# Values of an attention kernel cast to bf16 by their DMA instead of by an engine, in a kernel that interleaves attention with an MLP

## The chip, the cores and the metric

One core of a Trainium2 chip runs the whole program. The metric is the device time of one execution in microseconds (us), the median of several runs. Engines: PE is TensorE, DVE is VectorE, ACT is ScalarE, POOL is GpSimd, SP is SyncE; "PEld" is PE's weight load, and "SPq" or "POOLq" is an engine's queue of DMA issues.

## The reference, cut to what matters

Attention over 8 batches with 8 heads of 576 positions and 64 features, then an MLP with a gate over all 4608 tokens:

```python
scores = (1/8) * q @ k.T
mask_plain = (rel >= 0) & (rel < 32)                          # heads 0 to 3
mask_dil   = (rel >= 0) & (rel < 128) & (rel % 4 == 0)        # heads 4 to 7
attn = softmax(where(mask, scores, -1e9));   y = attn @ v      # per batch and head
x = y.transpose(0, 2, 1, 3).reshape(4608, 512)
h = x @ w_in                                                  # 512 -> 2048
out = (h * sigmoid(beta * h)) @ w_out                          # 2048 -> 512
```

## The kernel before

Matmuls are in bf16. The MLP works on nine tiles of 512 tokens; while tile t is at the MLP, attention of batch t+1 is done in the same instruction streams. What the two share out is fixed when the program is built: each attention step has a **weight**, and a step is put behind the next MLP slot (four matmuls) as soon as the share of weights done falls behind the share of slots done. Batches 0, 1 and 2 have step lists of their own; batches 3 to 7 share one.

```python
THIRD = ("d0 d1 v0 S20 S21 S22 k0 S23 v1 V20 S30 k1 V21 S31 q0 V22 ... V33 v2 S10 V00 ...").split()  # batch 2
WORK = {"S": 3, "V": 3, "X": 2, "d": 3, "K": 3, "Q": 3, "k": 0, "q": 0, "v": 1}
...
while work and done * total < whole * seen:       # seen: MLP slots passed; tile 0 (batch 1) goes by a count of steps
    m, name = work.pop(0)
    done += WORK[name[0]]
    ...                                           # extras tied to this step (loads, spreads)
    attention_step(b, name)
```

S is scores and exp, V is the product with the values, X is the transposition into `xT`, the input of the MLP. The values go through f32 staging tiles and a cast:

```python
vp_st = [const([P, 4, NI, D], FP32) ...]          # plain heads, staged
vd_st = const([P, 2, 4, C, D], FP32)              # dilated heads, staged
vp[i], vd[i]                                      # bf16, rows of 66: 64 values, a column of ones, padding

def cast_v(b, n, eng):                            # after load_vp / load_vd into the staging tiles
    if n == 2 or n > 3:
        copy_on(eng)(out=vp[b % 2][:, h, :, 0:D], in_=vp_st[b % 2][:, h])
    else:
        copy_on(eng)(out=vd[b % 2][0:K, f]...[:, :, 0:D], in_=vd_st[0:K, f]...)
```

In batches 3 to 7 POOL casts; in batch 2 ACT does all of it (the steps v0, v1, v2); in batches 0 and 1 DVE, POOL and ACT share it. From the MLP the argument needs only that the product of `w_in` and `xT` follows the X steps of the batch on PE, in order, and that one DVE instruction per 128 features makes the gate product `g`:

```python
def slot_h(t, fb):
    for kt in (2, 3, 0, 1):                       # dilated columns of xT first, then the plain ones
        nc.tensor.matmul(hps, lhsT=w_in_bf[:, kt, ...], rhs=xT[:, kt, t*512:(t+1)*512], ...)
    nc.scalar.activation(out=tnh, in_=hps, func=ACT.Tanh, scale=beta_half)
    nc.vector.scalar_tensor_tensor(out=g, in0=tnh, scalar=1.0, in1=hps, op0=add, op1=mult)
```

The softmax here doesn't subtract the row's maximum and nothing guards it: scores larger than these inputs give would overflow.

Of the kernel before, what the change touches and what calls it, by code (L numbers as in the profile page):

```python
# [8 lines left out]
FP32 = mybir.dt.float32  # L9
BF16 = mybir.dt.bfloat16  # L10
# [10 lines left out]
).split()  # L21

FIRST = (
    "W10 K2 W2 Q2 W2 K3 S20 S21 Q3 W1 S22 S23 z0 S30 S31 S32 S33 v0 W2 V20 V21 K0 W1 v1 V22 K1 V23 W1 Q0 "
    "V30 W1 V31 W1 X20 S00 V32 S01 V33 X21 S02 v4 S10 X30 S11 V00 S12 X31 V01 H0 v5 X00 V10 H1 X01 V11 X10 X11 "
    "z1 z2"
).split()
SECOND = (
    "K2 Q2 K3 Q3 v0 S20 v1 S21 S22 S23 K0 K1 S30 V20 S31 Q0 V21 S32 V22 S33 V23 V30 S00 "
    "V31 X20 v2 S01 V32 S02 V33 S10 X21 S11 V00 X30 S12 V01 X31 V10 X00 V11 X01 X10 X11"  # L30
).split()
THIRD = (
    "d0 d1 v0 S20 S21 S22 k0 S23 v1 V20 S30 k1 V21 S31 q0 V22 S32 q1 V23 S33 q2 q3 V30 X20 S00 V31 "
    "S01 X21 V32 S02 V33 v2 S10 V00 X30 S11 V01 S12 X31 V10 X00 V11 X01 X10 X11"
).split()


# [1 line left out]
def kernel(  # L39
# [10 lines left out]
    nc = tc.nc  # L50
    P = 128
    B, H, S, D = q.shape
# [4 lines left out]
    WIN = 32  # L57
    C = 4
    CT = S // C
    DQ = (96, 48)  # L60
    DK = (96, 80)
    DO = (0, 64)
    QT = 96
    NI = S // QT
# [35 lines left out]
    const = lambda shape, dt, name: const_pool.tile(shape, dt, name=name)  # L100
    w_in_bf = const([P, NKT, DFF], BF16, "w_in_bf")
    w_out_bf = const([P, NFB, HD], BF16, "w_out_bf")
    ident_f = const([NFB, NFB], FP32, "ident_f")
# [16 lines left out]
    pt = [const([P, pt_w[x] + 80], BF16, f"pt{x}") for x in range(4)]  # L120
    vp = [const([P, 4, NI, DV], BF16, f"vp{i}") for i in range(2)]
    vd = [const([P, 2, 4, C, DV], BF16, f"vd{i}") for i in range(2)]
    vp_st = [const([P, 4, NI, D], FP32, f"vp_st{i}") for i in range(2)]
    vd_st = const([P, 2, 4, C, D], FP32, "vd_st")


    k1 = [xT[:, 2 * i:2 * i + 2, 2 * S:2 * S + WIN + S] for i in range(2)]
# [21 lines left out]
    def zeros():  # L149
        nc.vector.memset(warm_w[:], 0.0)  # L150
        nc.vector.memset(warm[:], 0.0)
        for hf in range(2):
            nc.vector.memset(neg_d[hf][:], 0.0)
        nc.vector.memset(neg_p[:], 0.0)
        nc.vector.memset(qzd[0][64:128, 0], 0.0)
        nc.vector.memset(qzd[0][0:64, 1], 0.0)
        nc.vector.memset(vp_st[0][0:WIN, 0, 0], 0.0)
        for x in range(4):
            nc.vector.memset(pt[x][:, pt_w[x]:], 0.0)
        for x in range(2, 4):  # L160
            nc.vector.memset(pt[x][64:96, 8 * DQ[0]:8 * DQ[0] + 32], 0.0)
        for i in range(2):
            nc.vector.memset(vd[i][:, :, :, :, D:D + 1], 1.0)
            nc.vector.memset(k1[i][:, :, 0:WIN], 0.0)
            nc.vector.memset(vp[i][:, :, :, D:D + 1], 1.0)
        nc.vector.memset(plain_T["k"][:, 0:WIN // 2], 0.0)
# [28 lines left out]
    def build_neg_p():  # L195
        band(neg_p[:], QT, -WIN, -1, 0.0, -NEG)
        nc.gpsimd.memset(neg_p[0:WIN, 0], -NEG)
# [31 lines left out]
    def load_w_in(c0, c1):  # L229
        nc.gpsimd.dma_start(  # L230
            out=w_in_bf[:, :, c0:c1], in_=moe_w_in[:, c0:c1].rearrange("(c p) d -> p c d", p=P))

    def load_w_out(g):
        nc.gpsimd.dma_start(
            out=w_out_bf[:, g * 4:(g + 1) * 4, :],
            in_=moe_w_out[g * 4 * P:(g + 1) * 4 * P, :].rearrange("(c p) d -> p c d", p=P))
# [32 lines left out]
    def load_plain(b, kind):  # L269
        r0 = H * S if kind == "q" else 0  # L270
        dst = raw[b, kind] = plain_T[kind]
        c0 = WIN // 2 if kind == "k" else 0
        nc.sync.dma_start_transpose(
            out=dst[:, c0:c0 + 2 * S],
            in_=scratch[b][r0:r0 + 4 * S].rearrange("(a r) d -> a (r d)", r=2))

    def copy_on(eng):
        return eng.copy if eng is nc.scalar else eng.tensor_copy
# [20 lines left out]

    def load_vp_1(b, eng, n=0, m=4 * NI, p=0):  # L300
        eng.dma_start(
            out=vp_st[b % 2][:].rearrange("p h i d -> p (h i) d")[p:P, n:n + m],
            in_=bass.AP(tensor=v.tensor, offset=v[b, 0].offset + (QT * n - WIN + p) * D,
                        ap=[[D, P - p], [QT * D, m], [1, D]]))


    def load_vp(b, eng, n=0, m=4 * NI, p=0):
        st = vp_st[b % 2][:].rearrange("p h i d -> p (h i) d")
        for e in range(2):
            eng.dma_start(  # L310
                out=st[64 * e + p:64 * e + 64, n:n + m],
                in_=bass.AP(tensor=v.tensor,
                            offset=v[b, 0].offset + (QT * n - WIN + e + 2 * p) * D,
                            ap=[[2 * D, 64 - p], [QT * D, m], [1, D]]))

    def load_vd(b, eng):
        rows = v[b, 4:8].rearrange("h (t T) d -> t h (T d)", T=C)
        st = vd_st[:].rearrange("p f h T d -> p f h (T d)")
        for hf in range(2):
            eng.dma_start(out=st[0:DK[hf], hf], in_=rows[DO[hf]:DO[hf] + DK[hf]])  # L320


    def cast_v(b, n, eng):
        if n == 2 or n > 3:
            h = slice(0, 4) if n == 2 else slice(2 * n - 8, 2 * n - 6)
            copy_on(eng)(out=vp[b % 2][:, h, :, 0:D], in_=vp_st[b % 2][:, h])
        else:
            f, K = (slice(n, n + 1), DK[n]) if n < 2 else (slice(0, 2), 96)
            copy_on(eng)(  # L329
                out=vd[b % 2][0:K, f].rearrange("p f h T e -> p (f h T) e")[:, :, 0:D],  # L330
                in_=vd_st[0:K, f].rearrange("p f h T d -> p (f h T) d"))


    for b in range(2):
# [139 lines left out]
            nc.scalar.copy(out=o, in_=xp[:, 0:m * n].rearrange("p (T t) -> p T t", T=C))  # L474

    STEP = {"K": step_k, "Q": step_q, "S": step_s, "V": step_v, "X": step_x}
    BRING = {"d": spread_dil, "k": spread_k, "q": spread_q, "v": cast_v, "z": zeros_q}

    def attention_step(b, name):
        if name[0] == "W":  # L480
            for n in range(int(name[1:])):
                nc.tensor.matmul(warm_ps[:], lhsT=warm_w[:, 0:P], rhs=warm_w[:], start=True, stop=True)
        elif name[0] == "H":
            early[0] = -1
            slot_h(0, int(name[1:]), (2, 3))
        elif name[0] in STEP:
            STEP[name[0]](b, *[int(c) for c in name[1:]])
        else:
            eng = (nc.scalar if name[0] == "v" and (b, name) in ((1, "v2"), (2, "v0"), (2, "v1"), (2, "v2")) else
                   nc.gpsimd if b == 0 and name in ("v1", "v4", "v5") else nc.vector)  # L490
            BRING[name[0]](b, int(name[1:]), eng)


    g_t, o_t = {}, {}
# [89 lines left out]
    def extras(b):  # L584
        e = {}
        at = lambda name, fn, *a: e.setdefault(steps(b).index(name), []).append(lambda: fn(*a))
        V, A, G = nc.vector, nc.scalar, nc.gpsimd
        SQ = nc.sync
        if b + 1 < B:
            if b > 1:  # L590
                if b == 2:
                    at("S20", gate, raw[2, "q"][0:1, 0:1])
                for kind in "kq":
                    at("S20", cast_qk, b + 1, kind)
                at("X20", load_vd, b + 1, SQ)
                at("X20", load_vp, b + 1, SQ)
            if b == 1:
                at("X20", load_vd, b + 1, SQ)
                at("X20", load_vp, b + 1, SQ)
            if b > 1:  # L600
                for kind in "kq":
                    at("V21", load_dil, b + 1, kind)
                for kind in "kq":
                    at("V30", load_plain, b + 1, kind)
            if b > 1:
                at("S11", spread_dil, b + 1, 0, V)
                at("V01", spread_dil, b + 1, 1, V)
                at("X00", cast_v, b + 1, 3, G)
                at("X01", cast_v, b + 1, 2, G)
        return e  # L610


# [17 lines left out]
    load_tok(0, "q", 0)  # L630
    load_vp_1(0, G, 0, 1, WIN)
    load_vp_1(0, G, 1, 2 * NI - 1)
    load_vp_1(0, G, 2 * NI, 2 * NI)
    for name in FIRST:
        if name == "v1":
            attention_step(0, "v1")
            build_neg_p()
            for c0, c1 in ((0, 256), (256, 512), (512, 1024)):
                load_w_in(c0, c1)
            continue  # L640
        if name == "v5":
            load_w_in(1024, 2048)
            make_identity(nc, ident_f[:])
        if name == "X10":
            build_beta()
        attention_step(0, name)
    for x, g in ((1, 0), (0, 1)):
        for n in "kq":
            load_tok(1, n, x)
        load_w_out(g)  # L650
    G.memset(vd_st[64:96, 1], 0.0)
    load_vd(1, G)
    load_w_out(2)
    load_vp_1(1, G)
# [3 lines left out]
        load_dil(2, kind)  # L658
    for kind in "kq":
        load_plain(2, kind)  # L660
    load_w_out(3)
    zeros_kz()
    build_masks_d()
# [1 line left out]


    at_once = [3, 2] + [1] * (NTT - 3) + [4]
    WORK = {"S": 3, "V": 3, "X": 2, "d": 3, "K": 3, "Q": 3, "k": 0, "q": 0, "v": 1}
    left = []
    first = lambda n: max(0, n - 9) if n < 14 else 3 * n - 37  # L670
    for t in range(NTT):
        slots = []
        n = len(left)
# [59 lines left out]
```

## Time and profile before

| before | |
|---|---|
| median of the first 3 runs | 334.56 us (333.59 to 335.07) |
| span of the profiled run | 332.6 us |
| busy over the span: PE, ACT, DVE, POOL | 314.1, 199.3, 193.9, 131.4 us |
| V casts on POOL, from batch 3 on | 3.35 us a batch |

PE bounds the kernel; the stages, the waits of PE and the casts are shown line by line in the prediction. The profile's list of DMA queues shows one thing more (packets, MB, share of 16 engines' span): the uncast values of batches 2 to 7 went through q1 (those of batches 0 and 1 were issued from POOL and went through q0).

```profile
q1 hardware_dynamic: 57264, 25.58, 39.7%
q0 software_dynamic: 7632, 16.64, 27.5%
```

### The profile page before, as it was taken

The page shows a single profiled execution, that of the slowest core. Times are in us where ns is not written, and L with a number is a line of the kernel's source. Part 1 is how long each engine was busy: PE and PEld are TensorE (multiplying, and loading weights), DVE is VectorE, ACT ScalarE, POOL GpSimd, SP SyncE. Part 2 cuts the span into 40 slices and gives each one's busy share as a digit, 9 for nine tenths or more (in the row PEclk, how much of TensorE's full clock was granted, in tenths as well). Part 3 has the DMA queues.
Part 4 walks back from the last instruction along what each step waited for, and adds up shares of the span by engine and source line. Part 5 has one row for each costly group of instructions (what it writes and reads, how often), then busy time and mean ns, then how long its engine had stood idle before and what let it go on. Part 6 is the DMA issues. An engine that isn't in the chain of part 4 may idle for free.

```text
span 332.6 us, 6335 instructions
## 1 busy us (share of the span) xinstructions
PE 314.1 (94%) x2382; PEld 168.8 (51%) x2426; DVE 193.9 (58%) x432; ACT 199.3 (60%) x382; POOL 131.4 (39%) x172
## 2 busy tenths in 40 slices
PE   7798999987899899999999999999999999999995
PEld 3564466544455455555555555555555544444444
DVE  4558775479657775777376737673766344344400
ACT  3576756685757666666666666666666545355511
POOL 8792693133385346533653365335533000000000
PEclk9879999999999999999999999999999999999999
DMA  6999999998799795889597959792011210011131
GB/s 112 205 184 196 223 249 184 206 211 204 145 157 178 124 188 113 156 200 149 102 176 170 148 102 175 178 139 64 3 34 32 63 34 33 32 34 32 32 95 65
DMA packets 64927, 42.63 MB, mean 128 GB/s; under 512 B 48896, under 2 KB 58784, under 8 KB 64512
## 3 DMA queue, kind: packets, MB, share of 16 engines
q1 hardware_dynamic: 57264, 25.58, 39.7%
q0 software_dynamic: 7632, 16.64, 27.5%
q8 instruction: 19, 0.31, 0.4%
q14 instruction: 12, 0.10, 0.1%
HBM read 39.32 MB, written 16.52 MB: 168 GB/s over the span
## 4 chain that ended last, share of the span: by engine, by line
PE 84%; DVE 5%; ACT 3%; DMA 2%; POOL 2%; issue 2%; POOLq 0%; ACTq 0%; DVEq 0%
PE h_ps L505 31%; PE o_ps L543 27%; PE at L543 5%; PE at L443 4%; PE at L460 3%; PE at L505 3%; DVE g L515 2%; DMA xT<-in_k_dram 2%; PE h_ps L543 2%; PE at L410 2%; PE at L417 2%; ACT tnh L512 1%; PE at L358 1%; DVE qq L294 1%; PE at L559 1%
## 5 line engine op out<-in xcount | busy, mean ns | idle before, releaser
L515 DVE SCALAR_TENSOR_TENSOR g<-tnh,h_ps 128x512 bf16<-128x512 bf16 x130 | 88.7, 684 | 89.4 <-ACT tnh L512 88.8
L505 PE MATMUL h_ps<-xT,w_in_bf 128*128 128x512 bf16 x504 | 129.5, 379 | 3.2 <-DVE g L515 2.1
L512 ACT ACTIVATE tnh<-h_ps,beta_half 128x512 bf16<-128x512 f32 x130 | 89.4, 687 | 55.8 <-PE h_ps L505 51.6
L543 PE MATMUL o_ps<-w_out_bf,g 128*128 128x512 bf16 x429 | 109.3, 379 | 1.0
L505 PEld LDWEIGHTS <-w_in_bf 128*128 128x128 bf16 x576 | 51.8, 98 | 52.2 <-issue 4.1
L543 PEld LDWEIGHTS <-g 128*128 128x128 bf16 x560 | 50.2, 98 | 47.5
L425 POOL TENSOR_TENSOR pt<-pt,mask_d 96x384 bf16<-96x384 bf16 (+1 forms) x48 | 36.7, 775 | 49.9 <-ACT pt L423 49.3
L423 ACT ACTIVATE pt<-at 128x384 bf16<-128x384 f32 (+2 forms) x107 | 46.0, 439 | 17.0 <-PE at L410 8.6
L450 DVE TENSOR_TENSOR xs<-at,rcp 48x256 bf16<-48x256 f32 (+2 forms) x91 | 42.2, 463 | 8.8 <-PE at L460 4.7
L425 POOL TENSOR_TENSOR pt<-pt,mask_PP 128x384 bf16<-128x384 bf16 x24 | 22.8, 951 | 37.5 <-ACT pt L423 37.4
L443 PEld LDWEIGHTS <-pt 128*128 128x128 bf16 (+2 forms) x448 | 24.8, 99 | 15.3 <-DVE vd L329 1.2
L548 ACT ACTIVATE osb<-o_ps 128x512 f32<-128x512 f32 x28 | 16.7, 597 | 19.0 <-PE o_ps L543 18.7
L446 DVE RECIPROCAL rcp<-at 48x4 f32<-48x4 f32 (+2 forms) x91 | 16.0, 176 | 7.8 <-PE at L443 7.1
L417 PEld LDWEIGHTS <-kdT 128*96 128x96 bf16 (+1 forms) x128 | 14.3, 120 | 10.8 <-issue 1.4
L460 PE MATMUL at<-ident_b,xs 96*128 96x96 bf16 (+1 forms) x224 | 18.1, 200 | 1.6 <-DVE xs L450 1.0
L543 PE MATMUL at<-w_out_bf,g 128*128 128x512 bf16 x79 | 19.3, 379 | 0.1
L460 PEld LDWEIGHTS <-xs 96*128 96x128 bf16 (+1 forms) x224 | 13.4, 97 | 11.3 <-issue 2.1
L443 PE MATMUL at<-vd,pt 96*128 96x65 bf16 (+1 forms) x244 | 17.7, 196 | 0.7 <-DVE vd L329 0.7
L417 PE MATMUL at<-qzd,kdT 128*80 128x96 bf16 (+1 forms) x122 | 17.1, 226 | 1.0 <-DVE qzd L282 1.0
L425 POOL TENSOR_TENSOR pt<-pt,mask_FP 128x384 bf16<-128x384 bf16 x12 | 10.9, 912 | 16.1 <-ACT pt L423 16.1
L505 PE MATMUL at<-xT,w_in_bf 128*128 128x512 bf16 x54 | 13.5, 379 | 0.8 <-DVE kdT L371 0.4
L474 ACT COPY xT<-at 128x384 bf16<-128x384 bf16 (+1 forms) x32 | 12.7, 396 | 2.6 <-PE at L460 2.6
(115 smaller groups left out, 259.1 us busy)
## 6 DMA issues: line engine op xcount, KB each, us to landing
vp_st<-in_v_dram SPq DMA_DIRECT2D x12, 384.0 KB, 9.2
qk<-in_k_dram POOLq DMA_DIRECT2D x6, 576.0 KB, 6.1
qk<-in_q_dram POOLq DMA_DIRECT2D x6, 576.0 KB, 9.3
vd_st<-in_v_dram SPq DMA_DIRECT2D x6, 384.0 KB, 5.7
w_out_bf<-in_moe_w_out_dram POOLq DMA_DIRECT2D x4, 512.0 KB, 16.2
vd_st<-in_v_dram SPq DMA_DIRECT2D x6, 320.0 KB, 6.7
out_dram<-osb SPq DMA_DIRECT2D x7, 256.0 KB, 2.9
out_dram<-osb SPq DMA_DIRECT2D x8, 224.0 KB, 2.4
```

The costliest lines, as they stand in the source:

```text
L417: nc.tensor.matmul(sc[0:K, a, 0:2 * n], lhsT=kd[b][:, rp, h4, DO[hf]:DO[hf] + K], rhs=qzd[b % 2][:, :, rp, h4, hf * DQ[0]:hf * DQ[0] + n], ...
L423: nc.scalar.activation(out=w, in_=sc[0:K, :, 0:2 * n], func=ACT.Exp, scale=SCALE)
L425: nc.gpsimd.tensor_tensor(out=w, in0=w, in1=mask[0:K], op=ALU.mult)
L443: nc.tensor.matmul(pv[:, a, h2, :], lhsT=pt[x][0:K, c:c + P], rhs=rhs, start=True, stop=True)
L446: nc.vector.reciprocal(out=rcp[0:n, 0:m], in_=pv[0:n, :, :, D])
L450: nc.vector.tensor_tensor(out=xs_t[b, x, jx][:, a0:a0 + m], in0=pv[0:n, :, :, 0:D], in1=rcp[0:n, 0:m].unsqueeze(3).to_broadcast([n, m, 2, ...
L460: nc.tensor.transpose(xp[:, a * n:(a + 1) * n], xs[:, a].rearrange("p h d -> p (h d)"), ident_b[0:n, 0:n])
L505: nc.tensor.matmul(hps, lhsT=w_in_bf[:, kt, fb * P:(fb + 1) * P], rhs=xT[:, kt, t * NTOK:(t + 1) * NTOK], start=(kt == 2), stop=(kt == 1))
L512: nc.scalar.activation(out=tnh[:], in_=hps, func=ACT.Tanh, scale=beta_half[:, fb:fb + 1])
L515: nc.vector.scalar_tensor_tensor(out=g[:], in0=tnh[:], scalar=1.0, in1=hps, op0=ALU.add, op1=ALU.mult)
L543: nc.tensor.matmul(ops[:], lhsT=g_t[t, fb][:, tb * P:(tb + 1) * P], rhs=w_out_bf[:, fb, :], start=(fb == 0), stop=(fb == NFB - 1))
L548: nc.scalar.mul(out=osb[:], in_=ops[:], mul=0.5)
```

## The change

The intent is to rid the engines of the casts: a DMA can turn f32 into bf16 on its way. Plain heads go straight into the padded tile, whose row of 64 values is 128 B at a stride of 132 B, so a load becomes 3072 pieces (24 per partition, 128 partitions) of 256 B read and 128 B written. Dilated heads go as rows of 1 KB into a bf16 staging tile, and a copy ("spread") puts them into the padded tile. All these loads are now issued from POOL. The core of the diff:

```diff
-    vp_st = [const([P, 4, NI, D], FP32, f"vp_st{i}") for i in range(2)]
-    vd_st = const([P, 2, 4, C, D], FP32, "vd_st")
+    vd_st = [const([P, 2, 4, C * D], BF16, f"vd_st{i}") for i in range(2)]
 # load_vp, load_vp_1: out=vp[...][p:P, n:n + m, 0:D] instead of vp_st
-    def cast_v(b, n, eng): ...
+    def spread_v(b, hf, eng):
+        copy_on(eng)(out=vd[b % 2][0:K, hf]...[:, :, 0:D], in_=vd_st[b % 2][0:K, hf]...)
 # THIRD: the steps v0, v1, v2 are gone (SECOND loses v2, FIRST loses v4 and v5)
-    WORK = {..., "v": 1}
+    WORK = {..., "v": 0}
 # extras of batch b, for batch b + 1:
-                at("X20", load_vd, b + 1, SQ); at("X20", load_vp, b + 1, SQ)
-                at("X00", cast_v, b + 1, 3, G); at("X01", cast_v, b + 1, 2, G)
+            if b == 1:
+                at("X20", load_vp, b + 1, G)
+                at("X10", spread_v, b + 1, 0, A); at("X11", spread_v, b + 1, 1, A)
+            if b > 1:
+                at("X20", load_vd, b + 1, G); at("X20", load_vp, b + 1, G)
+                at("X00", spread_v, b + 1, 0, G); at("X01", spread_v, b + 1, 1, G)
 # start-up: w_in is issued without waiting for a cast of vd; vd of batch 2 goes ahead of w_out's last quarter
+    load_vd(2, G)
     load_w_out(3)
```

More of the change, by code (lines that the diff above doesn't have):

```diff
@@ L23 @@
 FIRST = (
-    "W10 K2 W2 Q2 W2 K3 S20 S21 Q3 W1 S22 S23 z0 S30 S31 S32 S33 v0 W2 V20 V21 K0 W1 v1 V22 K1 V23 W1 Q0 "
-    "V30 W1 V31 W1 X20 S00 V32 S01 V33 X21 S02 v4 S10 X30 S11 V00 S12 X31 V01 H0 v5 X00 V10 H1 X01 V11 X10 X11 "
+    "W10 K2 W2 Q2 W2 K3 S20 S21 Q3 W1 S22 S23 z0 S30 S31 S32 S33 v0 W2 V20 V21 K0 v1 W1 V22 K1 V23 W1 Q0 "
+    "V30 W1 V31 W1 X20 S00 V32 S01 V33 X21 S02 S10 X30 S11 V00 S12 X31 V01 H0 X00 V10 H1 X01 V11 X10 X11 "
     "z1 z2"
@@ L28 @@
 SECOND = (
-    "K2 Q2 K3 Q3 v0 S20 v1 S21 S22 S23 K0 K1 S30 V20 S31 Q0 V21 S32 V22 S33 V23 V30 S00 "
-    "V31 X20 v2 S01 V32 S02 V33 S10 X21 S11 V00 X30 S12 V01 X31 V10 X00 V11 X01 X10 X11"
+    "K2 Q2 K3 Q3 v0 S20 S21 v1 S22 S23 K0 K1 S30 V20 S31 Q0 V21 S32 V22 S33 V23 V30 S00 "
+    "V31 X20 S01 V32 S02 V33 S10 X21 S11 V00 X30 S12 V01 X31 V10 X00 V11 X01 X10 X11"
 ).split()
 THIRD = (
-    "d0 d1 v0 S20 S21 S22 k0 S23 v1 V20 S30 k1 V21 S31 q0 V22 S32 q1 V23 S33 q2 q3 V30 X20 S00 V31 "
-    "S01 X21 V32 S02 V33 v2 S10 V00 X30 S11 V01 S12 X31 V10 X00 V11 X01 X10 X11"
+    "d0 d1 S20 S21 S22 k0 S23 V20 S30 k1 V21 S31 q0 V22 S32 q1 V23 S33 q2 q3 V30 X20 S00 V31 "
+    "S01 X21 V32 S02 V33 S10 V00 X30 S11 V01 S12 X31 V10 X00 V11 X01 X10 X11"
 ).split()
@@ L156, in zeros @@
         nc.vector.memset(qzd[0][0:64, 1], 0.0)
-        nc.vector.memset(vp_st[0][0:WIN, 0, 0], 0.0)
+        nc.vector.memset(vp[0][0:WIN, 0, 0, 0:D], 0.0)
         for x in range(4):
@@ L301, in load_vp_1 @@
         eng.dma_start(
-            out=vp_st[b % 2][:].rearrange("p h i d -> p (h i) d")[p:P, n:n + m],
+            out=vp[b % 2][:].rearrange("p h i d -> p (h i) d")[p:P, n:n + m, 0:D],
             in_=bass.AP(tensor=v.tensor, offset=v[b, 0].offset + (QT * n - WIN + p) * D,
@@ L307, in load_vp @@
     def load_vp(b, eng, n=0, m=4 * NI, p=0):
-        st = vp_st[b % 2][:].rearrange("p h i d -> p (h i) d")
+        st = vp[b % 2][:].rearrange("p h i d -> p (h i) d")
         for e in range(2):
             eng.dma_start(
-                out=st[64 * e + p:64 * e + 64, n:n + m],
+                out=st[64 * e + p:64 * e + 64, n:n + m, 0:D],
                 in_=bass.AP(tensor=v.tensor,
@@ L317, in load_vd @@
         rows = v[b, 4:8].rearrange("h (t T) d -> t h (T d)", T=C)
-        st = vd_st[:].rearrange("p f h T d -> p f h (T d)")
         for hf in range(2):
-            eng.dma_start(out=st[0:DK[hf], hf], in_=rows[DO[hf]:DO[hf] + DK[hf]])
-    def cast_v(b, n, eng):
-        if n == 2 or n > 3:
-            h = slice(0, 4) if n == 2 else slice(2 * n - 8, 2 * n - 6)
-            copy_on(eng)(out=vp[b % 2][:, h, :, 0:D], in_=vp_st[b % 2][:, h])
-        else:
-            f, K = (slice(n, n + 1), DK[n]) if n < 2 else (slice(0, 2), 96)
-            copy_on(eng)(
-                out=vd[b % 2][0:K, f].rearrange("p f h T e -> p (f h T) e")[:, :, 0:D],
-                in_=vd_st[0:K, f].rearrange("p f h T d -> p (f h T) d"))
+            eng.dma_start(out=vd_st[b % 2][0:DK[hf], hf], in_=rows[DO[hf]:DO[hf] + DK[hf]])
+    def spread_v(b, hf, eng):
+        K = DK[hf]
+        copy_on(eng)(
+            out=vd[b % 2][0:K, hf].rearrange("p h T e -> p (h T) e")[:, :, 0:D],
+            in_=vd_st[b % 2][0:K, hf].rearrange("p h (T d) -> p (h T) d", T=C))
     for b in range(2):
@@ L476 @@
     STEP = {"K": step_k, "Q": step_q, "S": step_s, "V": step_v, "X": step_x}
-    BRING = {"d": spread_dil, "k": spread_k, "q": spread_q, "v": cast_v, "z": zeros_q}
+    BRING = {"d": spread_dil, "k": spread_k, "q": spread_q, "v": spread_v, "z": zeros_q}
     def attention_step(b, name):
@@ L488, in attention_step @@
         else:
-            eng = (nc.scalar if name[0] == "v" and (b, name) in ((1, "v2"), (2, "v0"), (2, "v1"), (2, "v2")) else
-                   nc.gpsimd if b == 0 and name in ("v1", "v4", "v5") else nc.vector)
-            BRING[name[0]](b, int(name[1:]), eng)
+            BRING[name[0]](b, int(name[1:]), nc.vector)
     g_t, o_t = {}, {}
@@ L589, in extras @@
         if b + 1 < B:
+            if b == 1:
+                at("X20", gate, raw[2, "q"][0:1, 0:1])
+                at("X20", load_vp, b + 1, G)
+                at("X10", spread_v, b + 1, 0, A)
+                at("X11", spread_v, b + 1, 1, A)
             if b > 1:
-                if b == 2:
-                    at("S20", gate, raw[2, "q"][0:1, 0:1])
                 for kind in "kq":
                     at("S20", cast_qk, b + 1, kind)
-                at("X20", load_vd, b + 1, SQ)
-                at("X20", load_vp, b + 1, SQ)
-            if b == 1:
-                at("X20", load_vd, b + 1, SQ)
-                at("X20", load_vp, b + 1, SQ)
+                at("X20", load_vd, b + 1, G)
+                at("X20", load_vp, b + 1, G)
             if b > 1:
@@ L607, in extras @@
                 at("V01", spread_dil, b + 1, 1, V)
-                at("X00", cast_v, b + 1, 3, G)
-                at("X01", cast_v, b + 1, 2, G)
+                at("X00", spread_v, b + 1, 0, G)
+                at("X01", spread_v, b + 1, 1, G)
         return e
@@ L632 @@
     load_vp_1(0, G, 1, 2 * NI - 1)
+    build_neg_p()
     load_vp_1(0, G, 2 * NI, 2 * NI)
+    for c0, c1 in ((0, 256), (256, 512), (512, 1024), (1024, 2048)):
+        load_w_in(c0, c1)
+    make_identity(nc, ident_f[:])
     for name in FIRST:
-        if name == "v1":
-            attention_step(0, "v1")
-            build_neg_p()
-            for c0, c1 in ((0, 256), (256, 512), (512, 1024)):
-                load_w_in(c0, c1)
-            continue
-        if name == "v5":
-            load_w_in(1024, 2048)
-            make_identity(nc, ident_f[:])
         if name == "X10":
@@ L650 @@
         load_w_out(g)
-    G.memset(vd_st[64:96, 1], 0.0)
     load_vd(1, G)
@@ L667 @@
     at_once = [3, 2] + [1] * (NTT - 3) + [4]
-    WORK = {"S": 3, "V": 3, "X": 2, "d": 3, "K": 3, "Q": 3, "k": 0, "q": 0, "v": 1}
+    WORK = {"S": 3, "V": 3, "X": 2, "d": 3, "K": 3, "Q": 3, "k": 0, "q": 0, "v": 0}
     left = []
```

## The prediction

> **What bounds the kernel now.** I read the summary first, then its 40 slices, then a table of busy time by stage, and only then the waits inside each stage. TensorE (PE) is busy 94% of the span, and the chain of work that ended last is 84% PE. So the question is not how much other work the change removes but where PE stands still. These are the stages (columns: stretch, its length, busy us with instruction counts of PE, PEld, DVE, ACT, POOL, then granted clock, DMA share, GB/s):
>
> ```profile
> 0.00:30.00 30.00, 24.41 (x279) 15.53 (x283) 17.04 (x61) 16.28 (x38) 21.57 (x41) 0.89 1.02 174
> 30.00:60.00 30.00, 28.90 (x292) 16.79 (x296) 20.85 (x44) 20.25 (x39) 17.91 (x26) 1.00 1.17 213
> 60.00:100.00 40.00, 34.99 (x282) 18.80 (x287) 26.34 (x58) 27.68 (x55) 17.08 (x21) 1.00 0.98 184
> 100.00:130.00 30.00, 28.47 (x229) 15.46 (x231) 22.12 (x48) 20.19 (x41) 15.17 (x17) 1.00 0.83 149
> 130.00:310.00 180.00, 178.58 (x1205) 92.33 (x1229) 104.39 (x218) 109.55 (x204) 59.63 (x68) 1.00 0.51 99
> 310.00:332.60 22.60, 18.74 (x102) 9.89 (x101) 3.18 (x5) 5.32 (x9) 0.00 (x0) 0.99 0.20 59
> ```
>
> PE stands still 5.6 us in the first 30 us, 1.1 in the next 30, 5.0 from 60 to 100, 1.5 from 100 to 130, only 1.4 in the 180 us after that, and 3.9 in the tail, where V has no part. The five steady batches (130 to 310) can therefore give nothing: any work taken from POOL or DVE there lies beside a PE that is 99% busy. All that V can touch is in the first 130 us, some 13 us of idle PE. A gain of 2% is 6.7 us, half of all that. The DMA share tells the second thing: it is above 1 (packets overlap on an engine) up to 60 us, so in the start-up the transfers stand in a queue, and anything that makes V dearer to move moves every later transfer.
>
> What PE waits for between 60 and 100 us (us in total, times, longest):
>
> ```profile
> PE h_ps L505 <- DVE g L515: 2.1, 3, 1.1
> PE at L460 <- DVE xs L450: 1.0, 2, 0.5
> PE at L417 <- DVE qzd L282: 1.0, 1, 1.0
> PE at L410 <- DVE qq L294: 0.4, 1, 0.4
> PE at L443 <- ACT vp L326: 0.2, 1, 0.2
> ```
>
> The first line is the PSUM bank of the first product, freed by DVE's gate, which waits for ACT's tanh. In this stage ACT also casts V of batch 2: three instructions. That is why the line stands there and not in the later batches, where POOL casts.
>
> **What the Trainium skill says.** "DMA: Bandwidth & Descriptors", section "Rules for kernel authors": a cast during DMA has to be issued from GpSimd. The trace agrees: every load with a cast is issued from POOLq, and the uncast V of batches 2 to 7 from SPq. So the change also moves 24 issues from SP's queue to POOL's. The same page, section "Issuing engines are not separate DMA queues": all issuers run on the same 16 engines and interleave; in the trace the DMA row is full whichever queue carries the bytes, so the move wins no bandwidth. The same page, "Specifications": transfers under 512 B fall below line rate. The change makes pieces of 128 B out of pieces of 256 B; no run yet shows a cast that small, so I extrapolate below. "GPSIMD Engine Reference", section "When to use GPSIMD": one-input elementwise work is roughly at line rate there; the trace has 1.03 us on POOL against 0.62 to 1.01 us on DVE for the same class of cast, which agrees roughly.
>
> **The change part by part.**
>
> *Casts and copies.* What the trace has for the casts that go or shrink (durations min/median/max in ns):
>
> ```profile
> L326 POOL CAST vp<-vp_st x7: 815/1466/1467, 17.3 to 227.0; 128x1536 bf16<-128x1536 f32 x5, 128x768 bf16<-128x768 f32 x2
> L326 ACT CAST vp<-vp_st x2: 1473/1474/1475, 55.6 to 90.0; 128x1536 bf16<-128x1536 f32 x2
> ```
> ```profile
> L329 POOL CAST vd<-vd_st x6: 1034/1887/1887, 12.8 to 225.2; 96x2048 bf16<-96x2048 f32 x5, 80x1024 bf16<-80x1024 f32 x1
> L329 ACT CAST vd<-vd_st x2: 1032/1032/1032, 69.1 to 74.0; 96x1024 bf16<-96x1024 f32 x1, 80x1024 bf16<-80x1024 f32 x1
> ```
>
> A steady batch loses 1.89 + 1.47 = 3.36 us of POOL, gains two spreads of 1024 elements at about 1.03 (POOL's time goes by elements, not bytes: a copy of 384 bf16 took 0.51, a cast of 768 took 0.82) and four DMA issues at 0.65 to 0.75 (measured: 0.67 for a half of vd, 1.43 for a whole vp). Sum: 2.06 + 2.8 - 3.36 = +1.5 us of POOL per batch. The issues fall between the last dilated mask and the first plain mask, where POOL idles 2 to 3 us now. So POOL is no gain and no loss: 0 us.
>
> *Batch 2 (66 to 100 us).* ACT loses 1.03 + 1.03 + 1.47 = 3.5 us of V casts. The waits that they feed are 2.1 (bank of h) and 0.2 (vp), and a share of the spread waits behind them. I credit **-2.4 us**.
>
> *Where the two spreads of batch 2 went.* The diff puts them on ACT at X10 and X11 of batch 1. Comparing the two programs' order on ACT, they stand directly ahead of the last two xT copies of batch 1. Now:
>
> ```profile
> 63.94 0.60 ACT L548 ACTIVATE osb<-o_ps 128x512 f32<-128x512 f32 x1 [0.47 <-PE o_ps L543]
> 64.43 1.00 ACT L466 COPY xT<-at 128x288 bf16<-128x288 bf16 x3
> 64.68 0.30 PE L460 MATMUL at<-ident_b,xs 96*128 96x96 bf16 x3 [0.52 <-DVE xs L450]
> 64.82 1.04 PE L505 MATMUL h_ps<-xT,w_in_bf 128*128 128x512 bf16 x4
> ```
>
> The copies end at 65.4, and the first PE matmuls of token tile 1 that read the plain columns follow at once. With two spreads of 1.03 ahead of them, less some 0.3 that fits in ACT's gaps, that copy ends about 1.8 us later and PE[...] waits: **+1.8 us**. This is the rival that I hold likeliest to eat the gain.
>
> *The transfers.* From the packet records of the trace, grouped by size, casts of 1024, 2048, 2304, 4096 and 36864 source bytes took 60, 98, 107, 173 and 1393 ns in the median: a line of 21 ns + 0.037 ns per source byte. A 256 B piece with a cast is then an estimate of 30 ns. Without a cast a 4096 B packet of sixteen such pieces took about 288, so 18 a piece. One vp has 128 x 24 = 3072 pieces: 3072 x 12 / 16 engines = 2.4 us more of packet time, about 2 us at the overlap of 1.17. A vd (704 rows of 1 KB) becomes 704 x 60 / 16 = 2.6 against about 3.0: slightly cheaper. V of batches 0 and 1 thus costs the queue about +4 - 0.5, and vd of batch 2 (2.6 / 1.17 = 2.2 us), now put ahead of the last quarter of w_out, comes on top: up to +5.7 us, less perhaps 2 us of slack spots in the queue (POOL waits for casts no longer). That last quarter lands now at 38.4 + 19.2 = 57.6:
>
> ```profile
> L234 POOL DMA_DIRECT2D w_out_bf<-in_moe_w_out_dram x1: 796/796/796, 38.4 to 38.4; - x1
> ...
> DMA to landing us min/median/max: 19.2/19.2/19.2
> ```
>
> and its first reader, the tenth group of four second products, starts at 59.84:
>
> ```profile
> 59.84 1.03 PE L543 MATMUL h_ps<-w_out_bf,g 128*128 128x512 bf16 x4
> ```
>
> The slack is 2.2 us. With the landing 3.5 to 5.7 later PE waits 1.3 to 3.5; some of it may be absorbed: **+1.7 us**.
>
> *Start-up.* POOL no longer waits 2 us for vd before it issues w_in, and the vd ahead of the plain keys is a little cheaper, so the keys (which PE awaits for 1.2 us at 14 us) come earlier: **-0.6 us**.
>
> Sum: -2.4 + 1.8 + 1.7 - 0.6 = +0.5 us, on 334.56: **335.0 us**.
>
> **The rivals.** First, a clear gain: the transfers stay hidden (small casts cost no more per piece than uncast ones, or the queue has more room than I think) and ACT has room for the spreads. For it speaks that PE waits directly for a DMA for under 3 us in the whole start-up; against it that the DMA share is above 1 all the way. Then -2.4 - 0.6, and some DVE time of batches 0 and 1: 331 to 332. Second, the DMA becomes the bound of the first 65 us: 128 B pieces at a stride of 132 B may cost well over 30 ns. At 45 ns two vp loads add 8 us, w_out's last quarter and the cast scratch of batch 2 come late, and PE waits 6 us or more: 340. For it speaks that no cast in this trace is under 1 KB of source; against it the smooth line of those there are. Third, POOL's in-order queue: an issue that waits for the eighth DMA before it, or for a late transpose, holds masks back. In steady batches those DMAs are long done, so I give it under 1 us.
>
> **Range and chances.** The two losses can each be 0 or double, the credit of batch 2 can be 1 to 3.5: 330.5 to 339.8 holds it 8 times in 10. Faster than 327.9 needs half of all idle PE time before 130 us, so 0.03; slower than 341.3 needs the second rival in full, so 0.07; within 2% 0.90.
>
> **What would show it.** In the changed profile: the stage from 130 us with the same PE idle of about 1.4 us; PE waiting for DVE's g at 78 to 87 us gone; two copies vd<-vd_st on ACT at 64 to 68 us, with PE idle before its first products of tile 1, released by ACT xT; a PE wait released by the w_out DMA near 60 us; packets of 128 B at about 30 ns. I am wrong if those small packets cost 20 ns or 45, if w_out still lands ahead of its reader, or if PE waits in the steady batches.

## The result, and the profile after

The changed kernel took **337.38 us** in the median of four runs (337.26 to 337.99), beside 334.07 us (332.79 to 335.07) for the kernel before in the same rounds. The ratio is 1.0105, with a 95% interval of 1.0065 to 1.0144: slower by about 1%, and within 2%. A ratio here is the mean time of one kernel's fast runs over that of the other's in the same rounds, so it is not quite the ratio of the medians.

Where did 3 us come from? Some matmul records are missing from the trace of before (2382 on PE against 2426 after), so idle time of PE from the two traces can't be compared. All 144 gate products on DVE are there in both traces, and they follow PE closely, so I take their start times as milestones. Stage A runs from tile 0's thirteenth gate product to tile 1's first, stage B from there to tile 2's first, stage C from there to tile 8's thirteenth:

| us | before | after | difference |
|---|---|---|---|
| up to tile 0's 13th gate product | 41.03 | 40.65 | -0.38 |
| A: to tile 1's first | 25.58 | 27.96 | +2.38 |
| B: to tile 2's first | 34.59 | 34.78 | +0.19 |
| C: to tile 8's 13th | 209.31 | 210.06 | +0.75 |
| sum | 310.52 | 313.45 | +2.93 |

Both profiled runs had the same 6.8 us of half clock at the start. Even so the first row is the weakest: the profiles of e1 and e2, whose edits do not touch the start-up and which had 3.4 us of half clock each, differ in it by 0.7 us.

The queues after, to be set beside those of before: q0 has nearly five times the packets, and the time of its packets rose from 27.5% to 49.2% of 16 engines' span; that of q1 fell from 39.7% to 22.8%.

```profile
q0 software_dynamic: 37440, 19.66, 49.2%
q1 hardware_dynamic: 34224, 16.53, 22.8%
```

Two stages after (columns as in the prediction's table): from 60 to 100 us ACT has lost 2 us of work, from 130 to 310 POOL has gained 7. PE gained from neither.

```profile
60.00:100.00 40.00, 33.54 (x286) 18.14 (x283) 25.50 (x58) 25.71 (x51) 20.53 (x27) 1.00 0.85 127
130.00:310.00 180.00, 179.16 (x1234) 92.12 (x1232) 104.57 (x220) 109.33 (x204) 66.73 (x81) 1.00 0.55 87
```

**Stage A: the spreads on ACT.** ACT's and PE's lines of the timeline of the changed kernel (start, us, engine, line, operation, operands, count, and in brackets the idle time before it and what ended it):

```profile
64.86 1.03 ACT L322 COPY vd<-vd_st 96x1024 bf16<-96x1024 bf16 x1
65.79 0.40 ACT L459 COPY xT<-at 128x288 bf16<-128x288 bf16 x1
66.08 1.05 ACT L322 COPY vd<-vd_st 80x1024 bf16<-80x1024 bf16 x1
67.03 0.40 ACT L459 COPY xT<-at 128x288 bf16<-128x288 bf16 x1
67.48 0.38 PE L496 MATMUL h_ps<-xT,w_in_bf 128*128 128x512 bf16 x1 [1.98 <-ACT xT L459]
```

Each spread stands ahead of one of the last two copies into `xT`. The second of those copies ends at 67.4, and PE, which needs its columns next, has stood for 1.98 us. PE also waits 0.4 us for an exp of ACT at an earlier point of this stage, which it did not before; that wait stays in e6.

**Stage B: other waits in place of the old ones.** PE's waits from 60 to 100 us (us in total, times, longest):

```profile
PE h_ps L496 <- ACT xT L459: 2.0, 1, 2.0
PE at L403 <- DVE qq L293: 1.5, 1, 1.5
PE h_ps L496 <- DVE g L506: 1.4, 3, 0.6
PE at L410 <- DVE qzd L281: 1.4, 1, 1.4
```

The wait for `g` fell from 2.1 to 1.4 us, but those for `qq` and `qzd`, two DVE copies of the queries, grew from 0.4 to 1.5 and from 1.0 to 1.4. How the longer wait for `qq` came about shows when the timelines around one such copy are laid side by side. Before:

```profile
82.66 1.03 PE L505 MATMUL h_ps<-xT,w_in_bf 128*128 128x512 bf16 x4
...
83.06 0.92 DVE L294 COPY qq<-qpT 64x1152 bf16<-64x1152 bf16 x2
```

After:

```profile
84.98 0.96 DVE L293 COPY qq<-qpT 64x1152 bf16<-64x1152 bf16 x2
...
86.00 0.34 PE L403 MATMUL at<-qq,kz 128*128 128x96 bf16 x4 [1.49 <-DVE qq L293]
```

The copies take as long as before. But before, a slot of four MLP matmuls (1.03 us) covered them; after, the scores that read `qq` come directly, with no slot between. The change took three steps with weight out of batch 2's list, and what stayed is placed by share of the weights, so it moved against the MLP slots.

**Stage C: waits that were not there.** PE's only wait from 130 to 310 us that exceeds 0.1 us; before there was none:

```profile
PE at L403 <- DVE qq L293: 0.8, 3, 0.3
```

It recurs once in each of tiles 3, 4 and 5, where the changed kernel loses 0.25 us each. One of them, from the timeline after:

```profile
146.06 1.42 POOL L318 DMA_DIRECT2D vd_st<-in_v_dram  x2
...
146.38 0.71 DVE L293 COPY qq<-qpT 64x1152 bf16<-64x1152 bf16 x1
...
147.15 0.34 PE L403 MATMUL at<-qq,kz 128*128 128x96 bf16 x4 [0.27 <-DVE qq L293]
```

The copy takes 0.71 us here and 0.46 before. What is new beside it is POOL, issuing the value loads.

**The transfers.** The last quarter of w_out was issued later and landed at 40.4 + 17.2 = 57.6 us, exactly where it landed before, and PE did not wait for it:

```profile
L233 POOL DMA_DIRECT2D w_out_bf<-in_moe_w_out_dram x1: 757/757/757, 40.4 to 40.4; - x1
...
DMA to landing us min/median/max: 17.2/17.2/17.2
```

In the packet records the new 128 B pieces took 32 ns in the median. At the start PE's wait for the plain keys fell from 1.17 us to 0.23:

```profile
12.82 0.65 PE L351 MATMUL h_ps<-ident_b,xT 64*64 64x64 bf16 x18 [0.23 <-DMA xT<-in_k_dram]
```

### The profile page after: what moved, and what is told of

Its sections match the earlier page's. It is cut to its first block, busy times and chain, and to the rows that moved or that the text cites. A ratio compares the mean times of both kernels' runs of the same rounds, so it can differ in the third digit from the quotient of the medians.

```text
span 335.5 us, 6366 instructions
## 1 busy us (share of the span) xinstructions
PE 317.6 (95%) x2426; PEld 169.1 (50%) x2426; DVE 194.3 (58%) x433; ACT 197.4 (59%) x380; POOL 141.1 (42%) x192
## 3 DMA queue, kind: packets, MB, share of 16 engines
q0 software_dynamic: 37440, 19.66, 49.2%
q1 hardware_dynamic: 34224, 16.53, 22.8%
## 4 chain that ended last, share of the span: by engine, by line
PE 82%; DVE 10%; ACT 4%; DMA 1%; issue 1%; POOL 0%; DVEq 0%; ACTq 0%; POOLq 0%
PE h_ps L496 30%; PE o_ps L534 26%; PE at L534 5%; DVE g L506 4%; PE at L436 4%; PE at L496 3%; PE at L453 3%; ACT tnh L503 2%; PE at L403 2%; DVE qq L293 2%; PE h_ps L534 2%; DVE xs L443 2%; PE at L410 2%; DMA xT<-in_k_dram 1%; PE at L351 1%
## 5 line engine op out<-in xcount | busy, mean ns | idle before, releaser
L496 PE MATMUL h_ps<-xT,w_in_bf 128*128 128x512 bf16 x520 | 130.9, 379 | 3.8 <-ACT xT L459 2.2
L534 PE MATMUL o_ps<-w_out_bf,g 128*128 128x512 bf16 x448 | 112.8, 379 | 0.0
L403 PE MATMUL at<-qq,kz 128*128 128x96 bf16 x144 | 12.1, 206 | 3.6 <-DVE qq L293 3.6
L318 POOL DMA_DIRECT2D vd_st<-in_v_dram x16 | 11.2, 702 | 10.1 <-DMA w_in_bf<-in_moe_w_in_dram 6.9
## 6 DMA issues: line engine op xcount, KB each, us to landing
w_out_bf<-in_moe_w_out_dram POOLq DMA_DIRECT2D x4, 512.0 KB, 17.2
```

The source lines that it names most:

```text
L403: nc.tensor.matmul(sc[:, a, h2 * n:(h2 + 1) * n], lhsT=kz[b % 2][:, h4, i].rearrange("p e u -> p (e u)"), rhs=qq[b % 2][:, h4, i].rearrang ...
L496: nc.tensor.matmul(hps, lhsT=w_in_bf[:, kt, fb * P:(fb + 1) * P], rhs=xT[:, kt, t * NTOK:(t + 1) * NTOK], start=(kt == 2), stop=(kt == 1))
L534: nc.tensor.matmul(ops[:], lhsT=g_t[t, fb][:, tb * P:(tb + 1) * P], rhs=w_out_bf[:, fb, :], start=(fb == 0), stop=(fb == NFB - 1))
```

## The experiments

My theory after this: three causes that have nothing to do with the cost of the small pieces, namely ACT's spreads (A), the lost weights (B), and POOL's DMA issues beside a DVE copy (C). The rival: the transfers. Under it, e1 to e3 would leave the times where they are, and one more such load would hurt.

The table gives the stretches of the runs that were also timed, in us. "Half clock" is where the granted clock was 0.5 after the start-up, for 3.4 us each time.

| | before | after | e1 | e2 | e3 | e6 | e9 | e10 |
|---|---|---|---|---|---|---|---|---|
| to tile 0's 13th gate product | 41.03 | 40.65 | 39.99 | 39.27 | 38.48 | 39.30 | 39.31 | 39.34 |
| A | 25.58 | 27.96 | 26.83 | 28.48 | 28.59 | 25.90 | 28.48 | 25.90 |
| B | 34.59 | 34.78 | 34.77 | 34.89 | 36.10 | 33.51 | 36.31 | 33.51 |
| C | 209.31 | 210.06 | 210.07 | 210.05 | 209.33 | 209.32 | 210.06 | 209.32 |
| half clock from (us) | none | none | none | 67.2 | 65.5 | none | 67.6 | none |

The first row follows the half clock at the start (6.8 us in before and after, none in e3, 3.4 in the others), so it says nothing about an edit.

### e1: the spreads of batch 2 earlier, on the same engine

```diff
-                at("X10", spread_v, b + 1, 0, A)
-                at("X11", spread_v, b + 1, 1, A)
+                at("S02", spread_v, b + 1, 0, A)
+                at("S10", spread_v, b + 1, 1, A)
```

> One part moved: the two copies vd<-vd_st of batch 2, which in the changed kernel stand on ACT directly ahead of the last two xT copies of batch 1 (ACT, 64.9 and 66.1 us), stand on ACT between score steps of batch 1 instead (S02 and S10, about 56 to 59 us), where ACT idles. Theory (the two copies are what delays token tile 1): PE's wait of 1.98 us for ACT xT disappears, the first gate product of tile 1 comes about 2 us earlier than in the changed kernel, and the time falls by 1.6 to 2.2 us, to about 335.3. Rival (the late start of tile 1 comes from the transfers, that is late V or weights): the wait stays under another name and the time stays at 337.4.

Measured: 334.94 us (333.48 to 335.91, 4 runs) beside 334.74 (332.56 to 335.79, 7 runs) of before; ratio 1.0009 (0.9946 to 1.0071). The wait for ACT's `xT` is gone. ACT's last two copies into `xT` now follow each other, and PE goes on:

```profile
64.94 0.70 ACT L459 COPY xT<-at 128x288 bf16<-128x288 bf16 x2
...
65.90 1.46 PE L496 MATMUL at<-xT,w_in_bf 128*128 128x512 bf16 x6
```

Stage A is 1.13 us shorter than after, not 1.98, because this run had a wait of 0.9 us for a gate product at 45 us, behind two DVE copies of `vd` that took 1.70 and 1.08 us beside POOL's memsets of `kz` (the first took 0.35 us at 11.8 us of the run after, where a DMA issue of POOL had begun 0.02 us before). In e6, where the spreads stand in the same places and that wait is absent, A is 25.90, within 0.32 of before. So the place of the two spreads costs the whole of that wait. (The 0.32 that stay were not tested. Batch 1's list lost a step as well, v2, and from 55 to 64 us the order on PE differs from that of before in all the edited runs.)

### e2: no-op steps keep the places of v0, v1 and v2 in batch 2

```diff
-    "d0 d1 S20 S21 S22 k0 S23 V20 S30 k1 ... S02 V33 S10 V00 ..."
+    "d0 d1 n0 S20 S21 S22 k0 S23 n1 V20 S30 k1 ... S02 V33 n2 S10 V00 ..."
-    WORK = {..., "v": 0}
+    WORK = {..., "v": 0, "n": 1}
 # attention_step: a name that starts with "n" does nothing
```

> The changed kernel with three empty steps of weight 1 in batch 2 at the places where the old casts of V stood. They emit no instruction; they only restore how attention steps and MLP slots are interleaved, and from batch 2 on the order on PE and DVE is that of the kernel before. Theory (batch 2 gained nothing because losing three weighted steps moved DVE's spreads of q and k ahead of other work, so that PE meets them with nothing between): PE's wait for DVE qq at 86 us (1.49) falls to about 0.3 and that for DVE qzd (1.37) to about 1.0, and with the ACT casts gone batch 2 wins 1.5 to 2.5 us; time about 335.5. Rival (batch 2 is bound by DVE's own work whatever the interleaving): under 0.5 us, 337.

Measured: 335.4 us (334.46 to 336.45); ratio 1.0033 (0.9982 to 1.0084). The order of batch 2 on PE and DVE, compared in the two traces, is then that of before, with the casts gone. PE's waits from 60 to 100 us for the two copies fell from 1.5 and 1.4:

```profile
PE at L403 <- DVE qq L293: 0.6, 1, 0.6
...
PE at L410 <- DVE qzd L281: 0.4, 1, 0.4
```

Stage B nevertheless measured 34.89 in the profiled run, the slowest of the four, no better than after. The reason is in the granted clock: this run fell to 0.5 for 3.4 us from 67.2 on, directly behind the 2 us wait for ACT that e2 leaves in place. The next runs were meant to tell whether B comes down without it.

### e3: the value loads of batches 3 to 7 two steps later

```diff
-                at("X20", load_vd, b + 1, G)
-                at("X20", load_vp, b + 1, G)
+                at("S01", load_vd, b + 1, G)
+                at("S01", load_vp, b + 1, G)
```

> Only the issues of V's four loads for batches 3 to 7 move on POOL's queue, from step X20 to step S01, behind the first plain mask and after DVE's last copy of q. Theory (in batches 4, 5 and 6 POOL's issues run beside that copy qq<-qpT and stretch it from 0.46 to 0.71 us; PE waits 0.25 us for it three times): those copies are back at 0.46 and the three waits are gone, time 0.7 us lower, 336.7. Rival (the longer copy comes from something else, say the transfers themselves): copies stay at 0.7 and the time at 337.4.

Measured: 336.52 us (335.95 to 336.9); ratio 1.0064 (1.0018 to 1.0111). Stage C is 209.33, as before (209.31), and PE waits for nothing over 0.1 us from 130 to 310. The same copy as above, in e3:

```profile
146.16 0.46 DVE L293 COPY qq<-qpT 64x1152 bf16<-64x1152 bf16 x1
...
146.67 0.34 PE L403 MATMUL at<-qq,kz 128*128 128x96 bf16 x4
```

Nothing but the time of the issues changed, and the copy has its 0.46 us back. So it was the issuing on POOL. The page "Advanced Engine Details and Errata" of the Trainium skill, section "VectorE Performance Modes", notes that the second SBUF port of VectorE is shared with GpSimd, and that GpSimd instructions and VectorE's two-port modes interfere. The trace agrees in kind: copies from bf16 to bf16 in SBUF are stretched, by POOL's memsets and mask products and, here, by its DMA issues. The page gives no size for it.

The traces do, and they show that running side by side is not enough. In the twelve profiles 173 copies of `qq`, `qzd` or `vd` begin while a POOL operation is under way. The 13 of them that began less than 0.25 us after the start of a DMA issue kept their usual time, such as the one at 84.98 in the run after (0.45 us; the issue began 0.17 us before). Of the other 160, all but three took their usual time or lasted until 0.2 to 0.3 us after that operation, whichever is longer: the issue that began 0.32 us before the copy at 146.38 ended 0.46 us into it, and the copy took 0.71. It fits that the same loads cost next to nothing in batch 2's stage, where the two copies beside them took 0.45 and 0.49 us.

The total stays above before because A and B stay, and B shows the half clock again (36.10).

### e6: all three edits together

> The three edits of e1, e2 and e3 together. If the three causes are separate, their gains add up: 2.0 + 1.5 + 0.7 = about 4 us under the changed kernel, 333.2, and so some 1 us under the kernel before (start-up gain 0.4 plus what the casts off ACT give in batch 2). If they are one cause seen three times (a late tile 1 that the others follow), the sum stays near e1's 335.3.

Measured: 332.12 us (330.91 to 333.89); ratio to before 0.9938 (0.9882 to 0.9995). All three stages fall into place at once: A 25.90, B 33.51, C 209.32. Stage B, now without the half clock, is 1.08 us below before and 1.26 below e1, which differs in B by the no-op steps alone (e3's edit touches batch 2's stage only through POOL's loads for batch 3). So the weights cost 1.3 us in B, and what the missing casts are worth there is 1.1 us.

### e4 and e5: one more load, with a cast and without, ahead of the last quarter of w_out

```diff
     load_vd(2, G)
+    G.dma_start(out=vx[:]...[:, :, 0:D],          # e4: vx bf16, rows of 66;  e5: vx f32, rows of 64
+        in_=bass.AP(tensor=v.tensor, offset=v[2, 0].offset - WIN * D, ap=[[D, P], [QT * D, 4 * NI], [1, D]]))
     load_w_out(3)
```

The data is never read; only the transfer counts.

> Measures the disputed cost by itself: the changed kernel with one more load of the plain heads of a V (3072 pieces of 256 B, cast to 128 B) into a scratch tile that nothing reads, issued just ahead of the last quarter of w_out, in the full queue of the start-up. My prediction's price (30 ns a piece over 16 engines, overlap 1.17): w_out's last quarter lands 4.9 us later than in the changed kernel (57.6 there), at 62.5, and PE waits for it. Rival (small pieces overlap twofold on an engine, as the packet records of the changed kernel suggest): 2.5 to 3.2 us later, about 60.5, little or no PE wait.

> The same extra load without the cast (the same 3072 pieces of 256 B into a float32 scratch tile, by the same queue). By the prediction's price 18 ns a piece, 3072 x 18 / 16 / 1.17 = 3.0 us later than in the changed kernel, so 1.9 us less than the cast one. Rival (a cast piece costs the queue no more than an uncast one): both land within 0.6 us of each other.

Measured (one look each, so their state is unknown): e4 344.3 us, e5 338.75, before 334.91 beside them. The last quarter of w_out landed 8.4 us later with the casting load (42.6 + 23.4 = 66.0, of which 2.2 us is that it was issued later) and 2.8 us later with the uncast one (41.3 + 19.1 = 60.4). PE's wait for it in e4:

```profile
PE h_ps L535 <- DMA w_out_bf<-in_moe_w_out_dram: 6.0, 1, 6.0
```

And in e5:

```profile
PE h_ps L535 <- DMA w_out_bf<-in_moe_w_out_dram: 0.3, 1, 0.3
```

This revived the rival: 3072 small casts may cost 8 us of queue. But then the change, which has two such loads ahead of w_out, would have landed w_out late, and it did not. In the packet records of e4, 2249 of the 3072 added pieces ran before 55 us and took 32 ns each in the median. The other 823 dragged on from 55 to 62 us, beside batch 2's DMA transposes, and took 85 ns in the mean; the pieces of w_out behind them came through until 66 us.

### e7: the casting load of e4, placed earlier, right behind the plain values of batch 1

> The extra cast load of e4 (3072 pieces into a scratch tile), now issued right behind V of batch 1, so that it runs at about 44 to 47 us, before any DMA transpose is under way. In e4 it held back w_out's last quarter by 8.4 us while running beside the transposes of batch 2. Theory (small cast pieces are cheap alone, 15 to 17 ns each over 16 engines, and dear beside transposes): w_out's last quarter lands about 3 to 3.5 us later than in the changed kernel, at 61, and PE waits at most 1 us for it. Rival (a cast load of 3072 pieces costs the queue 8 us anywhere): it lands at 65 or later and PE waits 5 us or more.

Measured (one look): 336.78 us. The last quarter of w_out landed at 41.3 + 18.0 = 59.3, only 1.7 us later, and PE did not wait for it. From 44 to 46 us the 16 engines moved almost nothing but these pieces, so their price can be read from the count of packets:

```profile
DMA packets 2441, 0.32 MB, mean 159 GB/s; under 512 B 2440, under 2 KB 2440, under 8 KB 2440
```

2440 pieces in 2 us on 16 engines is 16 x 2000 / 2440 = 13 ns each, though each lasts 32 ns: two to three are in flight on an engine at a time. (The DMA share of the changed kernel from 42 to 44 us is 2.58, against 1.17 before.) So the same load costs 1.7 us of landing in one place and 8.4 in another. That the neighbourhood of the transposes decides it fits both, but no run moved the transposes alone, and what makes the pieces slow there, no run shows.

### e9, e10, e8: repeats of after and e6, and e6 with POOL's memsets later

```diff
 # e8, on top of e6
-    zeros_kz()
     build_masks_d()
     build_masks_p()
+    zeros_kz()
```

> The changed kernel once more, unedited, in more rounds and on the chip of the next two. Theory: 3 us over the kernel before (ratio about 1.009), and, because PE stands still for 2 us at 65 us, some executions have a second stretch of half clock at 66 to 72 us that costs them 1 to 1.5 us more, as the profiles of e2 and e3 had. Rival (the half clock there was chance, unrelated to the wait): it shows as often in kernels without the wait.

> The kernel of e6 again, for a tighter interval against the kernel before. Theory: 1 to 2.5 us under the kernel before, ratio 0.993 to 0.997, no half clock after the start-up. Rival (e6's first result was lucky in its start-up clock): ratio 1.000.

> e6 with POOL's four memsets of kz moved behind the building of the masks. In the changed kernel and in e1 to e3 DVE's copies of V of batch 1 (43 to 47 us) take 1.0 to 1.7 us beside those memsets, where the same copy undisturbed at 11.8 us takes 0.35. If the memsets stretch the copies, these come down to 0.35 to 0.6 and PE's wait for g at 45 us (0 to 0.9 in the runs so far) is gone: 0 to 0.9 us better than e6. Rival (any POOL work does it, the mask building as well): copies stay at about 1 us and the time equals e6's.

Measured, on one chip beside 333.88 us of before (332.1 to 336.69, 10 runs; six runs each): the changed kernel again 337.41 (335.07 to 337.98; ratio 1.0081, 1.0026 to 1.0136), e6 again 332.11 (331.13 to 333.77; 0.9946, 0.9892 to 1.0000), e8 332.15 (331.1 to 333.24; 0.9937, 0.9889 to 0.9986). So both results came again; the repair's gain is small, with intervals that end at 0.9995 and 1.0000. e8 did what it was to do on DVE (both copies of `vd` took 0.42 us, in e10 0.41 and 1.08) but won no time over e10: the wait that e1 had there is absent in e10, so nothing hung on it.

e9 and e10 had the same half clock at the start, so their difference up to tile 8, 314.16 - 308.08 = 6.08 us, can be split: A 2.58 (the 2.0 of the wait for ACT, and a wait of 0.7 us for a gate product like that of e1, which e10 did not have), B 2.80, C 0.74, and -0.03 before A. B differs by more than the 1.27 that lie between after and e10 because e9 fell to half clock once more. One row of its stages (the granted clock is the third number from the end), directly behind the wait for ACT:

```profile
68.00:70.00 2.00, 2.00 (x7) 0.63 (x6) 1.17 (x2) 0.81 (x2) 0.00 (x0) 0.50 1.45 257
```

Such a stretch of 3.4 us came in four of the six profiles with the 2 us wait (e2, e3, e5, e9; not in after and e7), and e4 had 6.8 us of it around its 6 us wait; it came in none of the five without the wait (before, e1, e6, e8, e10). From B in e2 against e6 (34.89 - 33.51) and in e3 and e9 against after (36.10 and 36.31 - 34.78) it costs 1.3 to 1.5 us. The page "TensorE: Matmul & The Clock Gate", section "Why this matters for your kernels", warns of gaps above about 3 us; here a gap of 2 us was followed by it.

The traces also show why two of the six escaped. The clock records change only at whole multiples of 3.41 us from the first record. Cut each trace into such steps: from 25 to 320 us half clock followed every step in which PE stood still for 1.86 us or more (1.86 in e3, 1.97 in e2, e5 and e9, 2.42 and 3.41 in e4) and none with 1.80 or less. In after and e7 the edge of a step fell into the wait and cut the idle time into 1.08 and 0.99, and 0.74 and 1.33 us. So whether the wait costs the half clock as well depended on where it fell against these steps. That is a pattern over twelve profiles, not a test of the clock's rule: at the start-up and in the tail the count fails (one step of e8, at 324 us, had 1.99 us and kept its clock). And timed runs without a profile show their mean clock, not where it fell.

## Why the prediction was right or wrong

Its total, 335.0 us, was 2.4 below the measured 337.38; the range and the expected class held. That is partly luck: the 1.7 us charged for w_out never came and made up for two thirds of the 2.6 us missed in batch 2. Two of its own signs of being wrong appeared, w_out landing ahead of its reader and a wait of PE in the steady batches. The sum came about differently from the way it was written:

| term of the sum | predicted | measured |
|---|---|---|
| start-up | -0.6 | -0.38 |
| spreads of batch 2 on ACT | +1.8 | +2.38 (1.98 of it the named wait) |
| last quarter of w_out | +1.7 | 0 |
| batch 2 | -2.4 | +0.19 |
| POOL in the steady batches | 0 | +0.75 |
| sum | +0.5 | +2.93 |

- **Spreads on ACT: right**, in mechanism, place and size: two copies at 64 to 67 us ahead of the last `xT` copies, 1.98 us against 1.8. e1 shows it by moving them. Not foreseen: 3.4 us of half clock often follow the wait, for 1.3 to 1.5 us more.
- **Start-up: right in mechanism.** The keys' wait fell by 0.94 us of 1.17. The size, 0.38 us, is inside the scatter of this row.
- **w_out: wrong.** The failing step is "about 2 us at the overlap of 1.17". The duration of a small piece was extrapolated well (30 ns, measured 32). What went wrong was to turn it into queue time with the overlap of the large packets: small pieces overlap 2.1 to 2.6 times. At 13 ns a piece (3072 x 13 / 16 = 2.5 us, an estimate from e7's rate) a casting load costs the queue about what an uncast one did (3072 x 12.6 / 16 = 2.4 us, an estimate from before: batch 1's packets of sixteen such pieces took 243 ns in the mean at a DMA share of 1.21, so 243 / 16 / 1.21 = 12.6 ns a piece), so w_out landed at 57.6 us as before. (Three sums of the prediction here are a little off, without effect on this: 3072 x 12 / 16 is 2.3, not 2.4; 5.7 less 2 is 3.7, not 3.5; and at 45 ns two loads would add 8.9 us, not 8.) The second rival, DMA as the bound, fell for this kernel; e4 shows that it is real in another place.
- **Batch 2: wrong, and the dearest miss.** The failing step is "I credit -2.4 us": the waits that ACT's casts fed were taken for the gain, on the assumption that all else stays where it is. But the casts were steps with weights in a list that paces the stage. The wait for `g` did shrink, by 0.7 us, and was not gone as expected; removing the steps brought the query copies against the scores that read them. With the pace kept (e6 against before) the casts are worth 1.08 us, so the credit was also more than twice too large.
- **POOL: wrong by 0.75 us.** The prediction's own count of POOL's time, +1.5 us a batch, is near what the records give: one pair of issues for `vd` (1.42 us), one for `vp` (1.92) and two spreads of 1.03 make 5.4, less 3.35 for the casts is +2.05. It was rightly called time off the path. The failing step is "So POOL is no gain and no loss": it asked when POOL is free, not what POOL's work does to DVE beside it. The 0.75 us is three copies of `qq` that PE had to wait for, 0.25 us each. It was named as a sign of error ("if PE waits in the steady batches") but by another mechanism, POOL's in-order queue, of which nothing shows.

What stays open: the difference of the medians (3.3 and 3.5 us in two sets of rounds) is some 0.5 us above the +2.93 of the profiled pair. The half clock after the ACT wait is a candidate. The mean clocks fit it: in the last rounds five of the changed kernel's six runs had 0.987 to 0.990, as against 0.984 to 1.000 in ten of before, and at a mean clock of 1.000 the one changed run took 335.07 us, three of before 332.1 to 333.15 and one of e8 331.10. But these runs don't show where the clock fell (the 6.8 us at the start of the profiled run of after gave 0.990 as well), so it is argued, not shown.

So the idea of the change is worth a little here: e6, with the same DMA casts, takes 0.6% less time than the kernel before in three sets of four or six runs (0.9938, 0.9946, and 0.9937 as e8; the intervals end at 0.9995, 1.0000 and 0.9986). Moving only where the rest was put took away all of the 1% loss.

## What to carry to other kernels

When work goes away in a kernel interleaved by fixed weights, keep its weight in the list first (a step that does nothing) and measure; then repace on purpose. Put work that is moved to another engine where that engine is not the last before TensorE's next stage, and see that no POOL operation, DMA issues included, is half done when a VectorE copy starts that TensorE is about to read. Price a transfer by when it and those behind it land, in the place where it will run: the duration of one packet says little, as the same load cost 1.7 us in one place and 8.4 in another.

## What the Trainium skill lacked or had wrong

- "DMA: Bandwidth & Descriptors", section "Specifications", says that transfers under 512 B fall below line rate. Its section "Why small descriptors are slow (HBM only)" prices pieces this small, but not with a cast, and does not say that a piece's record in a trace is longer than its price: a 128 B piece with a cast lasted 32 ns, but 2440 of them passed 16 engines in 2 us, 13 ns each (e7). Nor does a page say what such pieces cost beside DMA transposes: 823 of them lasted 85 ns in the mean there, and one such load held a later transfer back 8.4 us, an uncast one 2.8 (e4, e5; one run each, cause not shown).
- "Advanced Engine Details and Errata", section "VectorE Performance Modes", has the interference of GpSimd and VectorE without a size, and speaks of instructions in general. "SBUF — State Buffer", section "SBUF: two separate sides", has DMA issues from GpSimd among them, but as what VectorE holds up. The runs show the reverse (a copy of 64x1152 bf16 went from 0.46 to 0.71 us, and back in e3), that memsets do more (a copy of 96x1024 from 0.35 to as much as 1.70 us), and that a copy begun less than 0.25 us after the start of a DMA issue was spared (13 of 13).
- "TensorE: Matmul & The Clock Gate", section "Why this matters for your kernels", warns of gaps above about 3 us. A gap of 2.0 us was followed by 3.4 us at half clock in four of six profiles here, at a cost of 1.3 to 1.5 us, and no profile without the gap had it after the start-up; 1.86 us of idle time within one 3.41 us step was enough.
